# A linear-attention and expert kernel: eight input loads at the start, preparations held back behind the first block inverse, and its results sent by two queues

## The chip, the core and the metric

The kernel runs on one core of a Trainium2 chip. A core has TensorE (PE in the profile, its weight loads PEld), VectorE (DVE), ScalarE (ACT), GpSimd (POOL) and SyncE (SP), which here only issues DMAs. Each engine works through its own instructions in order; they meet through semaphores. The metric is the device time of one execution in microseconds, lower is better; several executions give a median.

## The reference

For 4 batches and 8 heads of width 40, a 40 x 40 state runs over 768 tokens; its outputs, 3072 tokens of 320 values, go into 8 experts whose weights P come from a normalised gate:

```python
for t in range(S):
    y[:, :, t] = np.einsum('bhd,bhde->bhe', rt, state)
    Sa = np.einsum('bhde,bhe->bhd', state, at)
    state_decay = state * wt[:, :, None, :] - np.einsum('bhd,bhe->bhde', Sa, bt)
    state = state_decay + np.einsum('bhd,bhe->bhde', vt, kt)
...
P = np.exp(x @ w_gate - logits.max())
for _ in range(8):
    P /= P.sum(1, keepdims=True) + 1e-09
    P /= P.sum(0, keepdims=True) + 1e-09
    P *= N / E
...
for e in range(E):
    out += P[:, e:e + 1] * (np.maximum(x @ w1[e], 0.0) @ w2[e])
```

## The kernel before

The token recurrence is done in 12 chunks of 64 tokens (`c`), for 4 batches (`b`), 8 heads as 4 pairs (`p`) with two halves (`h`). So there are 48 pieces, numbered `cb = 4c + b`. In a chunk the recurrence becomes matrix products and the inverse of a 64 x 64 unit triangular matrix for each head. Three kinds of work come of it.

*Preparation* (`prep`), one for each piece, independent of the state. It loads the packed inputs `inp` (451.5 KB), forms the running products of the decays with two scans on VectorE (`q` L124, backwards; `g` L134, forwards), stores `g` to memory as `gd`, scales keys into `kb` (L147) and `a` into `ab` (L153, L154), and forms the triangular products `ll` (L159) and the transposes `kt` (L167) on TensorE. VectorE masks a part of `ll` into `sx` (L169); ScalarE copies the rest, negated, into `lt`, which is stored to memory as `ld` (L162 or L178). From preparation 6 on, `kb` and `ab` are made by GpSimd. A set of results (`sx`, `bb`, `cc`) has 20 buffers, so that 20 preparations can be done before the recurrence has used one. Some early preparations use the memory of sets not yet needed (`IN_MAP`, `KB_SETS`, tiles called `st`) for their inputs and for `kb` and `lt`.

*Block inverse*, one for a group of two chunks (8 preparations). The triangular matrices are cut into 128 blocks of 32 x 32, one to a partition (`load_lu`, `lu`), and VectorE inverts them in place with 38 instructions, from `flip_l` (L200) over multiply and reduce pairs (`pr`, L184 to L196) to the last copy in `finish` (L369). The inverse `un` and its transpose `tn` are stored as `ud` and `nd`; `tload` brings them back by chunk as diagonal blocks `tt` (L252) and as operands `t1`, `t2` (`td`, L246, L248); `tmat` makes the off-diagonal part on TensorE (`gp` L261, `op` L266). `un`, `lu` and `tn` have one buffer each.

*Recurrence* (`recur`), five steps for each piece, with the four batches staggered: `av`, `xc`, `pu` (needs `tt` of its chunk, L308), `pm` (L310, VectorE), `c2`, `ws`, then `y`, the new state `z` and its transpose `zt`.

The events of all three are sorted by due times, and a scheduler then fixes the order on each engine; nothing is reordered at run time. The last part, the experts, has a hand-written order. Its first weights and tokens load while the recurrence ends.

The lines the change touches: the load of `inp` (L118), the buffer counts of `g1`, `q`, `kb`, `lt`, the queues of the `ld` stores, `lu` loads, `nd` stores and `tt` loads, and `do_prep`. `NSX` is 20; `N_SP = 8` says how many `ld` stores go by SP.

Of the kernel before, what the change touches and what calls it, by code (L numbers as in the profile page):

```python
# [11 lines left out]
F32 = mybir.dt.float32  # L12
# [5 lines left out]
NB, NH, S, D = 4, 8, 768, 40  # L18
C = 64
NCH = S // C  # L20
NP = 4
R2 = 104
RL = 112
# [6 lines left out]
def attention(ctx, tc, d, xd, ps, pq, pt, gs, lg):  # L30
    nc = tc.nc
    pin = ctx.enter_context(tc.tile_pool(name="a_in", bufs=1))
# [33 lines left out]
    ab_b = [pin.tile([R2, NP, 128], F32, name=f"ab{i}") for i in range(2)]  # L66
    g1_b = [pin.tile([RL, NP, 65], F32, name=f"g1{i}") for i in range(1)]
    vz_b = [const.tile([RL, NP, 104], F32, name=f"vz{i}") for i in range(5)]
# [44 lines left out]
    zp = [None] * NB  # L113

    def prep(c, b, ld):
        cb = c * NB + b
# [4 lines left out]
        a_in = inp[:, 776:1032].rearrange("r (p t) -> r p t", p=NP)  # L121
        qr = pin.tile([RL, NP, 65], F32, name="q")
        q = qr[:, ::-1]
# [3 lines left out]
        g1 = rot("g1", g1_b)  # L127
# [11 lines left out]
        if cb < NKB:  # L139
            raw = raws[KB_SETS[cb % len(KB_SETS)]]  # L140
            kb = raw[0:R2, 0:512].rearrange("r (p k t) -> r p k t", p=NP, k=2)
            lt = raw[0:64, 512:1024].rearrange("r (p k t) -> r p k t", p=NP, k=2)
        else:
            kb = pin.tile([R2, NP, 2, 64], F32, name="kb")
            lt = pin.tile([64, NP, 2, 64], F32, name="lt")
        eng = nc.vector if cb < NFAST else nc.gpsimd
# [13 lines left out]
        if cb < NKB:  # L160
            nc.scalar.activation(out=lt, in_=ll[64:128], func=AF.Copy, scale=-1.0)
            (nc.sync if cb < N_SP else nc.scalar).dma_start(out=ld[GRP[c][1], :, b], in_=lt)  # L162
            kt = pt.tile([128, NP, 2, 64], F32, name="kt", tag="pt")
        else:
            kt = pq.tile([128, NP, 2, 64], F32, name="kt", tag="pq")
# [11 lines left out]
        if cb >= NKB:  # L177
            (nc.sync if cb < N_SP else nc.scalar).dma_start(out=ld[GRP[c][1], :, b], in_=lt)  # L178
        return dict(cc=cc, g=gd, sx=sx, bb=bb)
# [53 lines left out]
    def tload(c):  # L233
        tt = rot("tt", tt_b)
        tts[c] = tt
        ld, ud, nd = invs[GRP[c][0]]
        t1, t2, lb = td_b[0][0:64], td_b[0][64:128], lg_b[0][0:64]
        cc = GRP[c][1]
        q = [slice(h * 32, h * 32 + 32) for h in range(2)]
        u = [[slice(cc * 64 + blk * 32 + h * 16, cc * 64 + blk * 32 + h * 16 + 16) for h in range(2)]  # L240
             for blk in range(2)]
        for h in range(2):
            nc.sync.dma_start(out=lb[q[h], :, q[h]],
                              in_=ld[cc, 0:32].rearrange("j b p h s -> j (b p) h s")[:, :, h, 32:64])
        for h in range(2):
            nc.sync.dma_start(out=t1[q[h]], in_=nd[u[0][h]].rearrange("g j s -> j g s"))  # L246
        for h in range(2):
            nc.sync.dma_start(out=t2[q[h]], in_=ud[u[1][h]].rearrange("g j s -> j g s"))  # L248
        for h in range(2):
            for blk in range(2):  # L250
                r = slice(h * 64 + blk * 32, h * 64 + blk * 32 + 32)
                nc.sync.dma_start(out=tt[r, :, r], in_=ud[u[blk][h]].rearrange("g j s -> j g s"))  # L252

# [107 lines left out]
    vz_cur = [rot("vz", vz_b) for _ in range(NB)]  # L361
    preps, invs, tts = {}, {}, {}

# [4 lines left out]
    def finish(s, us):  # L368
        nc.vector.tensor_copy(out=tn[us, 16:32, 0:16], in_=un[us, 0:16, 16:32].rearrange("u c j -> u j c"))  # L369
        for o in range(0, us.stop, 64):  # L370
            nc.sync.dma_start(out=invs[s][1][o:o + 64], in_=un[o:o + 64])
            nc.sync.dma_start(out=invs[s][2][o:o + 64], in_=tn[o:o + 64])

    def load_lu(s, n):
        ld = invs[s][0]
        for cc in range(n):
            for blk in range(2):
                for h in range(2):
                    u0, r0 = cc * 64 + blk * 32 + h * 16, blk * 32
                    nc.sync.dma_start(  # L380
                        out=lu[u0:u0 + 16],
                        in_=ld[cc, r0:r0 + 32].rearrange("j b p h s -> (b p) j h s")[:, :, h, r0:r0 + 32])
# [8 lines left out]
    def do_prep(s, c, b, first):  # L391
        if first:
            start_seg(s)
        preps[c, b] = prep(c, b, invs[s][0])

    for c in range(NCH):
        for b in range(NB):
            for k in range(5):
                ev.append((5 * c + k + SKEW * b, step, (c, b)))
        t = 5 * c + 2 - T_LEAD  # L400
        ev.append((t - L_LEAD, tload, (c,)))
        for half in range(2):
            ev.append((t + 2 * SKEW * half, tmat, (c, half)))
# [32 lines left out]
KB_POOL = (1,2,3,4,5,6,7)  # L436
IN_SETS = (16, 15, 14, 13)
KB_SETS = (12, 11, 10, 9)
IN_SEQ = (16,15,14,13,0,0,16,15)
IN_MAP = dict(enumerate(IN_SEQ))  # L440
N_SP = 8
NKB = 6
# [393 lines left out]
```

## Time and profile before

| what | value |
|---|---|
| median of 3 runs | 1837.33 us (1833.14 to 1839.12) |
| profiled execution, own time | 1831.31 us |
| its span | 1829.5 us |
| mean granted TensorE clock | 0.958 |
| PE busy | 1729.6 us (95%) |
| DVE busy | 1370.8 us (75%) |
| ACT, POOL busy | 855.2 us (47%), 877.5 us (48%) |
| moved by DMA | 140.47 MB |

A timeline row of the profile gives start and duration in us, engine, line, operation, output and inputs, shapes and count, and in brackets how long the engine sat idle before and what ended that. A row of grouped instructions gives the count, busy time and mean duration in ns, and the idle time before. A row of stretches gives from and to, the length, and for each engine the busy time and the number of instructions. In the page's row of slices each digit is the busy share of a fortieth of the span in tenths; for PEclk it is the clock that TensorE was granted.

### The profile page before, as it was taken

The page shows a single profiled execution, that of the slowest core. Times are in us where ns is not written, and L with a number is a line of the kernel's source. Part 1 is how long each engine was busy: PE and PEld are TensorE (multiplying, and loading weights), DVE is VectorE, ACT ScalarE, POOL GpSimd, SP SyncE. Part 2 cuts the span into 40 slices and gives each one's busy share as a digit, 9 for nine tenths or more (in the row PEclk, how much of TensorE's full clock was granted, in tenths as well). Part 3 has the DMA queues.
Part 4 walks back from the last instruction along what each step waited for, and adds up shares of the span by engine and source line. Part 5 has one row for each costly group of instructions (what it writes and reads, how often), then busy time and mean ns, then how long its engine had stood idle before and what let it go on. Part 6 is the DMA issues. An engine that isn't in the chain of part 4 may idle for free.

```text
span 1829.5 us, 31656 instructions
## 1 busy us (share of the span) xinstructions
PE 1729.6 (95%) x11843; PEld 1701.8 (93%) x11843; DVE 1370.8 (75%) x2356; ACT 855.2 (47%) x1848; POOL 877.5 (48%) x851
## 2 busy tenths in 40 slices
PE   5479999999889999999999999999999999999999
PEld 4478889889879999999999999999999999999999
DVE  7876977974798867777686878977686877767676
ACT  6347767756643533434343434345343343424342
POOL 6545655721662626547191735007182644628160
PEclk8569999989899999999999999999999999999999
DMA  7467878766620101111020112201020111102001
GB/s 193 128 150 173 191 181 178 183 139 135 176 77 20 57 20 57 38 39 57 20 75 20 57 37 61 69 1 60 16 76 20 57 38 38 57 20 75 13 26 44
DMA packets 211759, 140.47 MB, mean 77 GB/s; under 512 B 162965, under 2 KB 193813, under 8 KB 211605
## 3 DMA queue, kind: packets, MB, share of 16 engines
q1 hardware_dynamic: 207925, 132.70, 27.9%
q10 hardware_dynamic: 3680, 5.74, 1.2%
q8 instruction: 94, 1.54, 0.4%
q14 instruction: 60, 0.49, 0.1%
HBM read 110.78 MB, written 27.61 MB: 76 GB/s over the span
## 4 chain that ended last, share of the span: by engine, by line
PE 77%; DVE 6%; DMA 4%; issue 4%; POOL 2%; SPq 2%; ACT 2%; ACTq 0%; POOLq 0%; DVEq 0%
PE op L647 36%; PE p L582 33%; PE xc L297 2%; DMA inp<-in_inp_dram 1%; PE ll L159 1%; PE pu L308 1%; PE c L315 1%; PE av L289 1%; DMA xs<-xd 1%; DVE g L134 1%; POOL ab L153 1%; PE op L266 1%; DVE hl L606 1%; DVE pr L193 1%; DVE q L124 1%
## 5 line engine op out<-in xcount | busy, mean ns | idle before, releaser
L582 PE MATMUL p<-xch,wh 128*128 128x384 f32 (+1 forms) x1792 | 605.3, 339 | 9.3 <-DVE sm L600 5.6
L603 ACT ACTIVATE hh<-sm 128x384 fp32r<-128x384 f32 x512 | 269.4, 526 | 725.4 <-DVE sm L600 725.4
L647 PE MATMUL op<-wh,hh 128*128 128x320 f32 x1536 | 476.5, 311 | 1.4 <-ACT hh L603 1.3
L647 PE MATMUL op<-wl,hh 128*128 128x320 f32 x1536 | 474.3, 309 | 0.0
L647 PE MATMUL op<-wh,hl 128*128 128x320 f32 x1536 | 466.7, 309 | 0.7 <-DVE hl L606 0.7
L528 POOL TENSOR_TENSOR wl<-ws,wh 128x640 fp32r<-128x640 f32 x60 | 103.1, 1718 | 606.1 <-ACT wh L526 605.8
L606 DVE SCALAR_TENSOR_TENSOR hl<-sm,hh 128x384 fp32r<-128x384 f32 x512 | 373.0, 762 | 2.3 <-ACT hh L603 2.0
L582 PEld LDWEIGHTS p<-xch,wh 128*128 128x128 f32 (+1 forms) x1792 | 337.4, 188 | 13.1 <-DVE sm L600 6.8
L582 PE MATMUL p<-xcl,wh 128*128 128x384 f32 x896 | 302.6, 338 | 0.0
L582 PE MATMUL p<-xch,wl 128*128 128x384 f32 x896 | 301.7, 337 | 0.0
L647 PEld LDWEIGHTS op<-wh,hh 128*128 128x128 f32 x1536 | 289.9, 189 | 2.2 <-ACT hh L603 2.2
L647 PEld LDWEIGHTS op<-wl,hh 128*128 128x128 f32 x1536 | 290.7, 189 | 0.0
L647 PEld LDWEIGHTS op<-wh,hl 128*128 128x128 f32 x1536 | 286.4, 188 | 1.1 <-DVE hl L606 0.9
L600 DVE TENSOR_TENSOR sm<-p,u 128x384 f32<-128x384 f32 x384 | 234.4, 620 | 8.8
L582 PEld LDWEIGHTS p<-xcl,wh 128*128 128x128 f32 x896 | 168.8, 188 | 0.0
L582 PEld LDWEIGHTS p<-xch,wl 128*128 128x128 f32 x896 | 168.6, 188 | 0.0
L600 DVE TENSOR_TENSOR sm<-p,p 128x384 f32<-128x384 f32 x128 | 71.3, 557 | 129.0 <-PE p L582 72.4
L600 DVE TENSOR_TENSOR p<-p,p 128x384 f32<-128x384 f32 x128 | 71.1, 556 | 101.2 <-PE p L582 100.6
L600 DVE TENSOR_TENSOR u<-p,p 128x384 f32<-128x384 f32 x128 | 70.7, 553 | 58.0 <-PE p L582 56.7
L536 POOL TENSOR_TENSOR wl<-ss,wh 128x512 fp32r<-128x512 f32 x60 | 89.8, 1497 | 30.8 <-ACT wh L533 26.7
L321 POOL TENSOR_TENSOR y<-ws,gl 104x256 f32<-104x256 f32 x48 | 43.1, 897 | 121.5 <-DVE ws L317 88.7
L159 PE MATMUL ll<-ab,kb 104*128 104x128 f32 x336 | 63.0, 345 | 37.2 <-POOL kb L147 16.7
(163 smaller groups left out, 2758.0 us busy)
## 6 DMA issues: line engine op xcount, KB each, us to landing
ws<-in_wts_dram SPq DMA_DIRECT2D x60, 832.0 KB, 4.5
inp<-in_inp_dram SPq DMA_DIRECT2D x42, 451.5 KB, 4.4
gd<-g SPq DMA_DIRECT2D x48, 113.8 KB, 2.8
gl<-gd SPq DMA_DIRECT2D x48, 113.8 KB, 2.9
vz<-in_v_dram SPq DMA_DIRECT2D x48, 112.0 KB, 3.3
xd<-y SPq DMA_DIRECT2D x24, 224.0 KB, 3.5
ld<-lt ACTq DMA_DIRECT2D x40, 128.0 KB, 2.7
rb<-in_r_dram SPq DMA_DIRECT2D x96, 48.0 KB, 2.9
```

What stands on the lines that cost most here:

```text
L124: nc.vector.tensor_tensor_scan(out=qr.rearrange("r p t -> r (p t)"), data0=w65[:, 260:0:-1], data1=one65, initial=0.0, op0=ALU.mult, op1=A ...
L134: nc.vector.tensor_tensor_scan(out=ge.rearrange("r p t -> r (p t)"), data0=w65[:, 0:260], data1=g1.rearrange("r p t -> r (p t)"), initial= ...
L159: nc.tensor.matmul(ll[:, p], lhsT=kb[:, p], rhs=ab[:, p], start=True, stop=True)
L297: nc.tensor.matmul(xc[h][:, p], lhsT=pp["sx"][:, p, h], rhs=f[:, p, h], start=True, stop=True)
L321: nc.gpsimd.tensor_tensor(out=y[0:R2, :, b % 2], in0=ws[:, :, 0:64], in1=gl[0:R2, :, 0:64], op=ALU.mult)
L528: g.tensor_tensor(out=wl[:, 0:640], in0=raw[:, 256:896], in1=wh[:, 0:640], op=ALU.subtract)
L536: g.tensor_tensor(out=lv[:, 3:7], in0=so[:, :, 0], in1=hv[:, 3:7, 0], op=ALU.subtract)
L582: nc.tensor.matmul(o, lhsT=w_, rhs=x_, start=(j == 0), stop=(j == 3))
L600: eng.tensor_tensor(out=out, in0=x, in1=y, op=ALU.add)
L603: nc.scalar.activation(out=hh[:, f, h], in_=sm[f][:, h], func=AF.Relu)
L606: v.scalar_tensor_tensor(out=hl[:, f, h], in0=sm[f][:, h], scalar=0.0, in1=hh[:, f, h], op0=ALU.max, op1=ALU.subtract)
L647: nc.tensor.matmul(ops[i], lhsT=a[:, h, cs], rhs=w_[:, cw], start=(f == 0 and h == 0 and j == 0), stop=(last and h == 1 and j == 2))
```

## The change

Inputs: the first eight preparations each get a buffer of their own at the start (six in memory of sets 16, 15, 14, 13, 18, 17, two in `inp`), where six were loaded at once and the seventh and eighth waited for the first two buffers. `g1`, `q`, `kb` and `lt` have two buffers instead of one. Preparations from `N_OPEN = 10` on are issued after the last copy of the first inverse, in VectorE's order. The queue of an `ld` store is named by its group: the first group's eight go by SP, all others by ScalarE, as `N_SP = 8` had it. Of the first group's traffic, half of the `lu` loads, the `nd` stores and chunk 0's `tt` loads go by ScalarE's queue, and chunk 0 is loaded between the two halves of the results. [...]

```diff
-    g1_b = [pin.tile([RL, NP, 65], F32, name=f"g1{i}") for i in range(1)]
+    g1_b = [pin.tile([RL, NP, 65], F32, name=f"g1{i}") for i in range(2)]
...
+    def send_l(c, b, lt, ld):
+        s, cc = GRP[c]
+        (nc.scalar if s else nc.sync).dma_start(out=ld[cc, :, b], in_=lt)
...
-        qr = pin.tile([RL, NP, 65], F32, name="q")
+        qr = pin.tile([RL, NP, 65], F32, name="q", bufs=2)
...
-            kb = pin.tile([R2, NP, 2, 64], F32, name="kb")
-            lt = pin.tile([64, NP, 2, 64], F32, name="lt")
+            kb = pin.tile([R2, NP, 2, 64], F32, name="kb", bufs=2)
+            lt = pin.tile([64, NP, 2, 64], F32, name="lt", bufs=2)
...
-            (nc.sync if cb < N_SP else nc.scalar).dma_start(out=ld[GRP[c][1], :, b], in_=lt)
+            send_l(c, b, lt, ld)
...
-                nc.sync.dma_start(out=tt[r, :, r], in_=ud[u[blk][h]].rearrange("g j s -> j g s"))
+                (nc.sync if c else nc.scalar).dma_start(
+                    out=tt[r, :, r], in_=ud[u[blk][h]].rearrange("g j s -> j g s"))
...
-        nc.vector.tensor_copy(out=tn[us, 16:32, 0:16], in_=un[us, 0:16, 16:32].rearrange("u c j -> u j c"))
+        last = nc.vector.tensor_copy(out=tn[us, 16:32, 0:16], in_=un[us, 0:16, 16:32].rearrange("u c j -> u j c"))
         for o in range(0, us.stop, 64):
             nc.sync.dma_start(out=invs[s][1][o:o + 64], in_=un[o:o + 64])
-            nc.sync.dma_start(out=invs[s][2][o:o + 64], in_=tn[o:o + 64])
+            (nc.sync if s else nc.scalar).dma_start(out=invs[s][2][o:o + 64], in_=tn[o:o + 64])
+            if s == 0 and o == 0:
+                first_inv.append(last)
+                tload(0)
...
-                    nc.sync.dma_start(
+                    (nc.scalar if s == 0 and h else nc.sync).dma_start(
                         out=lu[u0:u0 + 16],
...
-        preps[c, b] = prep(c, b, invs[s][0])
+        if c * NB + b < N_OPEN:
+            preps[c, b] = prep(c, b, invs[s][0])
+        else:
+            with tc.issue_after(first_inv[0].ins):
+                preps[c, b] = prep(c, b, invs[s][0])
...
-        ev.append((t - L_LEAD, tload, (c,)))
+        if c:
+            ev.append((t - L_LEAD, tload, (c,)))
...
-IN_SETS = (16, 15, 14, 13)
+IN_SETS = (16, 15, 14, 13, 18, 17)
-IN_SEQ = (16,15,14,13,0,0,16,15)
+IN_SEQ = (16, 15, 14, 13, 18, 17, 0, 0)
-N_SP = 8
+N_OPEN = 10
...
-    nc = _bacc.Bacc("TRN2", target_bir_lowering=False, num_devices=1)
+    nc = _bacc.Bacc("TRN2", target_bir_lowering=False, num_devices=1, dynamic_dma_scratch_size=1024)
```

What the scheduler makes of it is seen on two engines. VectorE in the middle of the first inverse, before (the scans are listed as SCALAR_TENSOR_TENSOR; the line numbers after the change are 4 to 5 higher):

```order
L187 TENSOR_REDUCE un<-pr 128x4x6
L134 SCALAR_TENSOR_TENSOR g<-inp,g_205 112x260
L184 TENSOR_TENSOR pr<-un,lu 128x196
L187 TENSOR_REDUCE un<-pr 128x4x7
L169 TENSOR_TENSOR st_159<-ll,cst 64x8x64
L204 COPY tn<-un 128x4x8x8
L193 TENSOR_TENSOR pr<-un,lu 128x512
L196 TENSOR_REDUCE gt<-pr 128x64
L124 SCALAR_TENSOR_TENSOR q<-inp,cst 112x260
L193 TENSOR_TENSOR pr<-gt,tn 128x512
L128 RECIPROCAL g_205<-q 112x4
L196 TENSOR_REDUCE un<-pr 128x8x8
```

and the same stretch now:

```order
L191 TENSOR_REDUCE un<-pr 128x4x6
L188 TENSOR_TENSOR pr<-un,lu 128x196
L191 TENSOR_REDUCE un<-pr 128x4x7
L208 COPY tn<-un 128x4x8x8
L197 TENSOR_TENSOR pr<-un,lu 128x512
L200 TENSOR_REDUCE gt<-pr 128x64
L197 TENSOR_TENSOR pr<-gt,tn 128x512
L200 TENSOR_REDUCE un<-pr 128x8x8
```

The instructions of preparations have left the inverse; of all that stood there (6 `q`, 7 `g`, 7 `sx`) one `sx` remains. VectorE at the end of the first inverse, before (`st_165` is the result of preparation 16):

```order
L369 COPY tn<-un 128x16x16
L124 SCALAR_TENSOR_TENSOR q<-inp,cst 112x260
L128 RECIPROCAL g_205<-q 112x4
L134 SCALAR_TENSOR_TENSOR g<-inp,g_205 112x260
L169 TENSOR_TENSOR st_165<-ll,cst 64x8x64
L200 COPY lu<-lu 128x2x8x8
```

and now (`st_159` and `st_160` are those of preparations 10 and 11):

```order
L374 COPY tn<-un 128x16x16
L128 SCALAR_TENSOR_TENSOR q<-inp,cst 112x260 x2
L132 RECIPROCAL g_201<-q 112x4
L132 RECIPROCAL g_202<-q 112x4
L138 SCALAR_TENSOR_TENSOR g<-inp,g_201 112x260
L138 SCALAR_TENSOR_TENSOR g<-inp,g_202 112x260
L173 TENSOR_TENSOR st_159<-ll,cst 64x8x64
L128 SCALAR_TENSOR_TENSOR q<-inp,cst 112x260
L132 RECIPROCAL g_201<-q 112x4
L138 SCALAR_TENSOR_TENSOR g<-inp,g_201 112x260
L128 SCALAR_TENSOR_TENSOR q<-inp,cst 112x260
L173 TENSOR_TENSOR st_160<-ll,cst 64x8x64
```

One preparation stood between the end of the first inverse and the start of the second (L200); now ten do, 10 to 19, together with the first three `pm` of the recurrence. In the second inverse stood 5 `q`, 4 `sx` and 4 `pm`, now 9 `q`, 10 `sx` and 5 `pm`; and the third inverse, whose first copy stood three `pm` behind the second's last copy, now begins just ahead of it. SP around the last loads of the first inverse, before (`gd_568` and `gd_603` are the `g` of preparations 8 and 9; the `ld` stores shown are those of preparations 6 and 7):

```order
L178 DMA ld<-lt 64x512
L243 DMA lg<-ld 32x16x32
L138 DMA gd_568<-g 112x260
L178 DMA ld<-lt 64x512
L118 DMA inp<-in_inp_dram 112x1032
L138 DMA gd_603<-g 112x260
L380 DMA lu<-ld 16x32x32 x4
```

and now (`gd_576` and `gd_611` are those of preparations 8 and 9; the loads behind them are for 10 and 11):

```order
L117 DMA ld<-lt 64x512
L142 DMA gd_576<-g 112x260
L142 DMA gd_611<-g 112x260
L122 DMA inp<-in_inp_dram 112x1032
L117 DMA ld<-lt 64x512
L122 DMA inp<-in_inp_dram 112x1032
L388 DMA lu<-ld 16x32x32 x2
```

The store of preparation 7 has moved behind the `g` of preparation 9 and the load for preparation 10, and the last `lu` loads behind that for 11; two of the four have gone to ScalarE's queue.

More of the change, by code (lines that the diff above doesn't have):

```diff
@@ L177, in prep @@
         if cb >= NKB:
-            (nc.sync if cb < N_SP else nc.scalar).dma_start(out=ld[GRP[c][1], :, b], in_=lt)
+            send_l(c, b, lt, ld)
         return dict(cc=cc, g=gd, sx=sx, bb=bb)
@@ L361, in attention @@
     vz_cur = [rot("vz", vz_b) for _ in range(NB)]
-    preps, invs, tts = {}, {}, {}
+    preps, invs, tts, first_inv = {}, {}, {}, []
     def start_seg(s):
```

## The prediction

> **What bounds the kernel now.** I read the page's forty slices first: VectorE (DVE) is fullest and the TensorE clock lowest in the first tenth of the span, before the expert matmuls begin.
>
> ```profile
> DVE  7876977974798867777686878977686877767676
> PEclk8569999989899999999999999999999999999999
> ```
>
> Then I cut the attention stage at six rows of VectorE's timeline: start and end of the first block inverse (L200 to L369), start and end of the second, and the `pm` products that open chunk 2 and chunk 4.
>
> ```profile
> 56.32 0.27 DVE L200 COPY lu<-lu 128x128 f32<-128x128 f32 x1 [0.61 <-DMA ld<-lt]
> 97.53 0.57 DVE L369 COPY tn<-un 128x256 f32<-128x256 f32 x1
> 106.28 0.27 DVE L200 COPY lu<-lu 128x128 f32<-128x128 f32 x1 [4.23 <-DMA td<-nd]
> 148.34 0.37 DVE L369 COPY tn<-un 128x256 f32<-128x256 f32 x1
> 184.41 0.58 DVE L310 TENSOR_TENSOR pm<-pu,cst 128x416 f32<-128x416 f32 x1
> 251.89 0.56 DVE L310 TENSOR_TENSOR pm<-pu,cst 128x416 f32<-128x416 f32 x1
> ```
>
> The table of these stretches (busy time of PE, PE weight load, DVE, ACT, POOL, then granted clock, DMA share, GB/s) says which engine limits each:
>
> ```profile
> 56.30:98.10 41.80, 16.84 (x74) 14.70 (x72) 39.78 (x66) 15.75 (x40) 25.68 (x27) 0.50 0.46 125
> 98.10:106.30 8.20, 5.52 (x24) 4.90 (x24) 2.29 (x6) 3.34 (x10) 4.10 (x5) 0.50 0.84 177
> 106.30:148.70 42.40, 37.82 (x329) 35.98 (x330) 39.15 (x70) 24.43 (x61) 23.48 (x23) 0.79 0.71 148
> 148.70:184.40 35.70, 32.76 (x318) 31.24 (x317) 20.07 (x46) 24.92 (x65) 15.59 (x23) 0.97 0.77 177
> 184.40:251.90 67.50, 63.08 (x618) 60.10 (x617) 54.41 (x94) 49.92 (x126) 37.91 (x45) 0.96 0.83 188
> 251.90:420.00 168.10, 155.60 (x1442) 149.11 (x1442) 138.35 (x235) 116.32 (x295) 87.70 (x101) 0.91 0.75 166
> ```
>
> VectorE fills 95% of the first inverse and 92% of the second; from 148.7 us on TensorE is the fuller one (92%, 93%, 93%). So the first inverse is the bound where it stands, but what follows is a nearly full machine: a head start survives only as far as the work pushed behind it fits into idle time.
>
> **Step 1, until the first inverse can start** (now 56.3 us). Inputs of preparations 6 and 7 no longer wait for a buffer, and `kb`, `lt`, `q` are double. That removes two VectorE waits for `kb`, 2.02 and 1.62 us:
>
> ```profile
> 44.48 0.70 DVE L124 TENSOR_TENSOR_SCAN q<-inp,cst 112x260 f32<-112x260 f32 x1 [2.02 <-POOL kb L147]
> 48.92 0.70 DVE L124 TENSOR_TENSOR_SCAN q<-inp,cst 112x260 f32<-112x260 f32 x1 [1.62 <-POOL kb L147]
> 49.15 0.45 SPq L178 DMA_DIRECT2D ld<-lt  x1
> 51.40 1.93 SPq L380 DMA_DIRECT2D lu<-ld  x4
> ```
>
> Against it: in SP's new order the store of preparation 7 (now at 49.15) stands behind the `g` stores of 8 and 9 and the input load of 10, and the last `lu` loads behind that of 11. These wait for inputs of 8 and 9, which land 4.4 us after GpSimd has finished 6 and 7 and freed their buffers. Two of the four `lu` loads go by ScalarE's queue, half of 1.93 us. The extra `memset` of the second `g1` costs no more than the memsets in front of it, under 0.5 us. If only the gains counted the start would be 7 us earlier (49); if SP's new order eats them all, 56. I take 52, the middle: **-4**.
>
> **Step 2, the first inverse** (now 41.8 us). Its own multiply and reduce rows:
>
> ```profile
> 56.30:98.10 41.80, 24.73 (x34) 0.50 0.46 125
> ```
>
> Five transposing copies come on top, at most 0.57 each (L369), about 2.2 together, and one `sx` product (0.67) that stays between: 27.6 us. The seven preparations that shared the stretch go behind it. Bounds: 26 to 32. **-14**, so it ends at 79.6 instead of 98.1.
>
> **Step 3, from there to the second inverse** (now 8.2 us). In VectorE's new order preparations 10 to 19 all stand here, with three `pm`. One preparation, in the rows of its input tile (min/median/max ns):
>
> ```profile
> L124 DVE TENSOR_TENSOR_SCAN q<-inp,cst x42: 662/699/1187, 26.1 to 365.4; 112x260 f32<-112x260 f32 x42
> L134 DVE TENSOR_TENSOR_SCAN g<-inp,g x42: 676/698/1678, 29.3 to 369.4; 112x260 f32<-112x260 f32 x42
> L153 POOL TENSOR_TENSOR ab<-inp,g x40: 670/676/2702, 46.2 to 371.1; 40x256 f32<-40x256 f32 x40
> L154 POOL TENSOR_TENSOR ab<-inp,g x40: 673/855/2380, 47.0 to 371.8; 40x256 f32<-40x256 f32 x40
> L147 POOL TENSOR_TENSOR kb<-inp,q x40: 1171/1182/3429, 47.7 to 369.7; 104x512 f32<-104x512 f32 x40
> DMA to landing us min/median/max: 3.3/4.4/11.0
> ```
>
> There are still two `inp` buffers. A buffer goes round in 4.4 (landing) + 0.7 (`q`) + 0.7 (`g`) + 1.5 (`ab` twice) = 7.3 us, and about 8.5 with issue, reciprocal and the neighbour's 1.2 us `kb` in between. 10 and 11 are there, done 5 us after the inverse; four more pairs at 8.5 make 39; last `g` and the `lu` loads 4 more: 43 us. Lower bound, GpSimd alone: 10 x (1.18 + 0.68 + 0.86 + about 0.2) = 29. Upper bound: today's pace between 56.3 and 98.1, seven in 41.8, or 6.0 each: 60. The SP loads stand in pairs behind `g` stores, so I stay with the buffer round: **+35**. Second inverse at 122.6 instead of 106.3.
>
> Inside this step chunk 0 gets its blocks back. `nd` and the four `tt` loads go by ScalarE:
>
> ```profile
> 98.13 1.08 SPq L372 DMA_DIRECT2D nd<-tn  x2
> 105.35 2.08 SPq L252 DMA_DIRECT2D tt<-ud  x4
> 106.90 1.91 PE L261 MATMUL gp<-td,lg 64*64 64x32 f32 x16 [0.73 <-DMA td<-nd]
> 113.67 2.03 PE L308 MATMUL pu<-x,tt 128*128 128x104 f32 x8
> ```
>
> That takes 3.2 us of issue off SP, while the 16 transfer engines are at 0.84 already. But the first `pu` now stands on TensorE behind `ll` and `kt` of preparation 12, whose input is a round late, so it still comes some 16 to 19 us after the inverse, as now (15.6): it is hidden, and I cost the second queue at nothing; were that cover gone, the 3.2 us would come off step 3, and were the landings halved too, some 2 us more. [...]
>
> **Step 4, the second inverse** (now 42.4 us, 5 `q`, 4 `sx`, 4 steps inside). The new order has 9 `q`, 10 `sx` and 5 to 6 steps inside. Rows of that stretch:
>
> ```profile
> L290 DVE TENSOR_TENSOR f<-av,cst 104x512 f32<-104x512 f32 x4 | 2.7, 669 | 1.4 <-PE av L289 1.4
> L169 DVE TENSOR_TENSOR sx<-ll,cst 64x512 f32<-64x512 f32 x4 | 2.7, 667 | 0.0
> L317 DVE TENSOR_TENSOR ws<-c,c 104x416 f32<-104x416 f32 x4 | 2.3, 571 | 0.0
> L310 DVE TENSOR_TENSOR pm<-pu,cst 128x416 f32<-128x416 f32 x4 | 2.3, 563 | 0.0
> ```
>
> Added: 4 `q` and 4 `g` at 0.70, 4 reciprocals at 0.17, 6 `sx` at 0.67, one `f`, one `pm`, two `ws`: 12.7 us, about 11 after the overlap of neighbours (39.15 busy of some 44 summed). **+11**, 53 us (49 to 58).
>
> **Step 5, to chunk 2's `pm`** (now 35.7, with 15.6 us of VectorE idle). The third inverse's inputs are already there, so 23 of its rows stand here: all of its multiply and reduce rows but the twelve large ones, and a copy.
>
> ```profile
> 106.30:148.70 42.40, 24.02 (x34) 0.79 0.71 148
> L193 DVE TENSOR_TENSOR pr<-un,lu 128x1024 f32<-128x1024 f32 x3 | 3.6, 1209 | 0.0
> ```
>
> 24.0 (the second inverse's rows) - 12 x 1.2 = 9.6, the copy 0.4; 2 `q`, 4 `g`, 2 `sx` and reciprocals 6; overlapped as above 14, plus a wait that I estimate at 3 us for `un` to be stored (ending at 148.7, the store must land before the next inverse overwrites it; landings here take 3 to 4): 17 us (14 to 21). **-19**.
>
> **Step 6, to chunk 4's `pm`** (now 67.5). TensorE bounds it. Four of eight preparations are done earlier:
>
> ```profile
> 99.25 2.08 PE L159 MATMUL ll<-ab,kb 104*128 104x128 f32 x8 [4.09 <-POOL ab L154]
> 155.84 1.08 PE L159 MATMUL ll<-ab,kb 104*128 104x128 f32 x8
> 156.75 0.52 PE L167 MATMUL kt<-cst,kb 104*128 104x104 f32 x4
> ```
>
> 4 x 1.60 = 6.4 at the warm rate: **-6** (56 to 66).
>
> **Step 7, the rest.** At chunk 4 the new order has one more preparation through TensorE (1.6 us) and 12 more inverse rows plus two `q` through VectorE (about 9 us). Both engines are near full there, so between -1.6 and -9: **-5**. The experts start later or sooner by the same amount; their 1.3 ms are untouched. [...]
>
> Sum, unrounded: -4.3 - 14.2 + 34.8 + 10.6 - 18.7 - 6.4 - 5 = -3.2. Against the profiled execution's 1831.3 us that is 1828; the median before is 6 us higher, 1837.3, so **1834.0**. A difference under 0.3%, 5.5 us, can't be told from none here.
>
> **Rivals.** *The head start survives (faster).* Step 3 runs at GpSimd's pace: 33 us. For it: landings as short as 3.3 and two of every buffer; against it: SP's in-order waits. Then -13, of which the full stages keep some: 1824.
> *The held preparations are the new wait (slower).* Step 3 keeps today's 6.0 us each, 60 us, +17; chunk 2 and the third inverse follow, and later idle time gives about 5 back: 1846. It decides from 5.2 us per preparation, step 3 over 52 us. For it: today's pace, and TensorE idle and unwarmed in front of it.
> *TensorE stays cold (slower).* The granted clock is 0.50 until 106 us; 10 preparations bunched with the first steps at 2.08 instead of 1.08 for `ll` cost 1.4 us each with `kt`. Six of them on the path: +8, 1842. Against it: the clock rose to 0.79 in today's second inverse.
> *VectorE is not alone in the inverse.* `g` took up to 1678 ns against a median of 698. If GpSimd's products of preparations 8 to 10 still run beside the inverse and lengthen its rows in that way, step 2 takes its upper 32: +4, 1838, within the no-change band. [...]
>
> **Chances.** Forecast 0.40, its own range 1827 to 1841; survives 0.28; new wait 0.18; cold 0.10; not alone 0.04. Faster by over 0.3%: 0.12 of the forecast and 0.26 of the first rival, 0.38. Slower: 0.16 of the new wait, 0.05 of the cold and 0.02 of the forecast's tail, 0.23. Within: 0.39. The range reaches from the first rival's far side, 1820, to the second's, 1848, leaving 0.1 on each side.
>
> **What would show it.** L204 (L200 now) at 52; its last copy 27 us later with a single foreign row; the second inverse near 123; `pm` of chunk 2 near 193 and of chunk 4 near 253. Wrong if the ten held preparations take under 35 or over 52 us, if VectorE still idles 15 us between the second and third inverse, or if the `pu` of chunk 0 comes within 10 us of the inverse's end.

## The result, and the profile after

| what | before | after |
|---|---|---|
| median | 1836.78 us (1833.14 to 1839.12, 4 runs) | 1866.15 us (1861.72 to 1868.70, 4 runs) |
| ratio, 95% interval | | 1.0152 (1.0118 to 1.0186) |
| span of the profiled execution | 1829.5 us | 1866.8 us |
| mean granted TensorE clock | 0.958 | 0.950 |

The change makes the kernel 1.5% slower, 29 us by the medians and 37 by the two profiled executions, of which the one before lies 5 us under its median and the one after 3 us over; the forecast was 3 us faster. The slices of the page of after show the place. In the second, which holds the first inverse, GpSimd falls to 2 tenths, where it had 5 before, and the clock is at 5 as it was. In the fifth the clock is down again to 6, where it had 9:

```profile
DVE  6759758767488877686777768887676867767675
POOL 6257436551365337182553718005381835538170
PEclk9579678999979999999999999999999999999999
```

GpSimd's row before, for comparison (the other two stand in the prediction):

```profile
POOL 6545655721662626547191735007182644628160
```

The same six rows of VectorE's timeline as in the prediction (line numbers 4 to 5 higher): start and end of the first inverse, start and end of the second, the `pm` that open chunks 2 and 4.

```profile
62.06 0.27 DVE L204 COPY lu<-lu 128x128 f32<-128x128 f32 x1 [6.78 <-DMA lu<-ld]
88.50 0.37 DVE L374 COPY tn<-un 128x256 f32<-128x256 f32 x1
141.21 1.22 DVE L204 COPY lu<-lu 128x128 f32<-128x128 f32 x1 [1.25 <-DMA lu<-ld]
197.48 0.34 DVE L374 COPY tn<-un 128x256 f32<-128x256 f32 x1
221.60 0.56 DVE L315 TENSOR_TENSOR pm<-pu,cst 128x416 f32<-128x416 f32 x1
295.10 0.58 DVE L315 TENSOR_TENSOR pm<-pu,cst 128x416 f32<-128x416 f32 x1
```

The stretches between them, and the last one on to the last `pm` (busy time of PE, its weight load, DVE, ACT and POOL; then clock, DMA share, GB/s):

```profile
62.10:88.90 26.80, 0.00 (x0) 0.00 (x0) 25.66 (x41) 1.09 (x3) 0.00 (x0) 0.50 0.02 5
88.90:141.20 52.30, 40.65 (x314) 38.34 (x315) 27.26 (x45) 29.36 (x73) 31.49 (x44) 0.74 0.83 181
141.20:197.80 56.60, 42.88 (x385) 40.51 (x383) 52.32 (x94) 42.41 (x108) 37.81 (x43) 0.91 0.72 181
197.80:221.60 23.80, 17.40 (x112) 16.45 (x112) 16.04 (x36) 7.08 (x18) 9.95 (x13) 0.56 0.66 148
221.60:295.10 73.50, 68.88 (x542) 65.81 (x542) 47.64 (x86) 41.01 (x106) 25.75 (x34) 0.77 0.62 136
295.10:540.20 245.10, 226.22 (x2133) 215.99 (x2132) 169.56 (x288) 165.09 (x405) 111.95 (x130) 0.93 0.71 161
```

Read it row by row. The first inverse is as short as meant, 26.8 us, but TensorE and GpSimd do nothing at all in it (x0), and the transfer engines are 2% busy. Then VectorE, which had been the bound, is busy only 27.3 of 52.3 us, while the ten held preparations go round. The second inverse takes 56.6. Chunk 2's `pm` comes 37.2 us later than before (221.60 against 184.41), and in these two executions nothing of it comes back: the spans differ by 37.3.

The late start of the first inverse (62.06, not 56.32) has its own cause:

```profile
42.11 0.57 SPq L122 DMA_DIRECT2D inp<-in_inp_dram  x1
47.42 0.70 DVE L128 TENSOR_TENSOR_SCAN q<-inp,cst 112x260 f32<-112x260 f32 x1 [6.89 <-DMA inp<-in_inp_dram]
51.39 0.59 ACT L177 ACTIVATE lt<-ll 64x512 f32<-64x512 f32 x1 [5.68 <-DVE sx L173]
52.89 0.45 SPq L117 DMA_DIRECT2D ld<-lt  x1
```

VectorE stands 6.89 us in front of the `q` of preparation 8, whose input went out at 42.11. Behind it stands `sx` of preparation 7 (50.71), behind that ScalarE's `lt` of 7, and behind that, at 52.89, the last store that the inverse needs. That store goes out 3.7 us later than before (49.15); the other 2.0 us of the late start lie behind it, where it takes 4.1 us to land and the last `lu` loads 4.2 to 4.4.

### The profile page after: what moved, and what is told of

Same layout as the page of the kernel before. It is cut to its first block, busy times and chain, and to the rows that moved or that the text cites. A ratio compares the mean times of both kernels' runs of the same rounds, so it can differ in the third digit from the quotient of the medians.

```text
span 1866.8 us, 31645 instructions
## 1 busy us (share of the span) xinstructions
PE 1739.9 (93%) x11843; PEld 1712.9 (92%) x11843; DVE 1366.1 (73%) x2357; ACT 855.6 (46%) x1848; POOL 865.9 (46%) x851
## 4 chain that ended last, share of the span: by engine, by line
PE 73%; DVE 3%; DMA 1%; issue 1%; POOL 0%; SPq 0%; ACT 0%; DVEq 0%; ACTq 0%; POOLq 0%
PE op L660 35%; PE p L595 33%; PE xc L302 1%; PE pu L313 1%; PE c L320 1%; PE av L294 1%; DVE hl L619 1%; PE op L271 0%; DVE sm L613 0%; DMA ws<-in_wts_dram 0%; PE zt L340 0%; PE gp L266 0%; PE lp L350 0%; DMA inp<-in_inp_dram 0%; DVE u L613 0%
## 5 line engine op out<-in xcount | busy, mean ns | idle before, releaser
L163 PE MATMUL ll<-ab,kb 104*128 104x128 f32 x336 | 59.6, 329 | 66.2 <-POOL ab L158 55.5
L163 PEld LDWEIGHTS ll<-ab,kb 104*128 104x128 f32 x336 | 51.4, 232 | 70.0 <-POOL ab L158 57.2
```

The lines of the kernel that those rows point to most:

```text
L163: nc.tensor.matmul(ll[:, p], lhsT=kb[:, p], rhs=ab[:, p], start=True, stop=True)
```

## The experiments

All times are medians, the ratios against the kernel before, run beside each. The columns: start of the first inverse, first `pm` of chunk 2, and from chunk 4's first `pm` to the last (length and granted clock), all from the one profiled execution of each, so that some us of a stretch can be that execution's own. Each kernel also has its own order from the scheduler; where two kernels differ by a few us, that order can be the reason as well as the edit's own subject, and no run separates the two.

| kernel | median us | ratio (95%) | inverse 1 | chunk 2 | chunk 4 to last |
|---|---|---|---|---|---|
| before | 1836.8 | | 56.3 | 184.4 | 248.8 at 0.91 |
| after | 1866.2 | 1.0152 (1.0118 to 1.0186) | 62.1 | 221.6 | 245.2 at 0.93 |
| hold_alone | 1844.9 | 1.0048 (1.0024 to 1.0073) | 56.1 | 209.9 | 239.7 at 0.92 |
| no_hold | 1842.7 | 1.0033 (1.0016 to 1.0050) | 59.5 | 196.1 | 251.8 at 0.91 |
| hold_from_16 | 1845.3 | 1.0051 (1.0031 to 1.0071) | 59.2 | 192.2 | 252.5 at 0.91 |
| hold_from_8 | 1865.0 | 1.0161 (1.0136 to 1.0186) | 51.8 | 222.9 | 242.9 at 0.93 |
| one_queue | 1874.9 | 1.0190 (1.0155 to 1.0225) | 61.9 | 227.3 | 248.3 at 0.91 |
| hold_8_behind_flip | 1876.1 | 1.0202 (1.0170 to 1.0233) | 53.5 | 225.2 | 257.7 at 0.87 |
| start_first_no_hold | 1854.0 | 1.0086 (1.0053 to 1.0118) | 51.8 | 195.3 | 256.3 at 0.86 |
| fill_idle | 1863.0 | 1.0128 (1.0101 to 1.0155) | 60.8 | 222.5 | 243.2 at 0.92 |
| queue_alone | 1839.6 | 1.0012 (0.9993 to 1.0031) | 56.7 | 183.4 | 256.4 at 0.88 |
| eight_loads_alone | 1852.9 | 1.0090 (1.0071 to 1.0109) | 58.4 | 192.8 | 249.5 at 0.92 |
| single_buffers | 1843.0 | 1.0030 (1.0011 to 1.0049) | 59.1 | 211.9 | 237.2 at 0.93 |
| three_inputs | 1865.9 | 1.0170 (1.0148 to 1.0193) | 59.6 | 218.0 | 263.0 at 0.85 |
| qg_double | 1867.8 | 1.0152 (1.0112 to 1.0191) | 60.6 | 219.4 | 260.2 at 0.87 |
| kb_lt_double | 1852.0 | 1.0071 (1.0043 to 1.0099) | 56.0 | 214.9 | 241.1 at 0.94 |
| no_hold_single | 1851.9 | 1.0076 (1.0050 to 1.0101) | 57.7 | 190.4 | 256.7 at 0.90 |
| hold_and_queue | 1849.9 | 1.0072 (1.0049 to 1.0095) | 56.3 | 207.6 | 241.6 at 0.92 |
| fill_longer | 1872.1 | 1.0172 (1.0136 to 1.0207) | 61.7 | 221.9 | 254.0 at 0.90 |
| hold_from_13 | 1844.1 | 1.0031 (1.0012 to 1.0051) | 57.3 | 195.5 | 248.1 at 0.89 |

**Which half of the change costs.** *no_hold*, the change with nothing held:

```diff
-N_OPEN = 10
+N_OPEN = 48
```

> The whole change but the hold (N_OPEN = 48: no preparation waits for the first inverse). Theory A, the ten held preparations that run at 5.2 us each between the inverses are the cause: without them the time goes back to 1830 to 1843, the first inverse is long again (about 40 us, preparations inside) and the second begins within 10 us of its end. Theory B, the new start (eight loads at once, pairs of q and g in front of the first inverse) is the cause, since the first inverse begins at 62.1 where it began at 56.3: the time stays at 1855 or more. Theory C, the second queue and chunk 0 first: stays at 1855 or more too. Both A and B expect the first inverse to begin at 60 to 63.

*hold_alone*, the kernel before with only the hold:

```diff
-        preps[c, b] = prep(c, b, invs[s][0])
+        if c * NB + b < N_OPEN:
+            preps[c, b] = prep(c, b, invs[s][0])
+        else:
+            with tc.issue_after(first_inv[0].ins):
+                preps[c, b] = prep(c, b, invs[s][0])
```

> The kernel before with the hold alone (preparations 10 on behind the first inverse's last copy); inputs, buffers and queues as before. Theory A: the first inverse begins near 56, lasts 27, the second begins 45 to 55 us behind its end, and the time is 1855 to 1870. Theories B and C: within 5 us of the time before, 1832 to 1842.

Neither theory holds alone. Without the hold 1842.7, the hold alone 1844.9: 6 and 8 us, where both together make 29. The rows say where they add and where they don't. Timeline of hold_alone:

```profile
82.51 0.37 DVE L369 COPY tn<-un 128x256 f32<-128x256 f32 x1
133.39 0.27 DVE L200 COPY lu<-lu 128x128 f32<-128x128 f32 x1 [3.13 <-DMA lu<-ld]
209.91 0.58 DVE L310 TENSOR_TENSOR pm<-pu,cst 128x416 f32<-128x416 f32 x1
```

and of no_hold:

```profile
196.05 0.56 DVE L315 TENSOR_TENSOR pm<-pu,cst 128x416 f32<-128x416 f32 x1
```

Theory A's forecast for no_hold came true (1830 to 1843); for hold_alone the time lies between the forecasts. Up to chunk 2's `pm` the two add up in these executions: 25.5 us from the hold (209.91 - 184.41), 11.6 from the rest, 37.2 together in after. With the old buffers and inputs the hold's ten preparations also take 50.5 us (82.9 to 133.4), nearly as long as in after. What differs is behind: the kernel with the hold alone wins 8 us back in the rest of the recurrence (308.3 us from chunk 2's `pm` to the last, before 316.3), after loses 2 more (318.7).

*hold_from_16* and *hold_from_8*, other limits of the hold in the change:

```diff
-N_OPEN = 10
+N_OPEN = 16   # hold_from_8: 8
```

> The change with the hold from preparation 16 on (N_OPEN = 16), so that the second inverse's own eight preparations stand beside the first inverse and the second begins right behind it in VectorE's order. Theory A in the form that the ten preparations bunch between the two inverses: most of the loss goes, 1830 to 1845. Theory A in the form that any idling of TensorE and GpSimd during the first inverse costs: 1845 to 1860. Theories B and C: 1855 or more.

> The change with the hold from preparation 8 on (N_OPEN = 8): twelve preparations held, and nothing of 8 and 9 in front of the first inverse. Theory A: two more held at 5.2 us, less some 5 us from an earlier first inverse (its last stores no longer stand behind q and g of 8 and 9): 1866 to 1876, the first inverse at 52 to 57. Theory B: the start is mended, and the time falls by what the inverse begins earlier, to 1856 to 1862.

From 16 on the second group stands beside the first inverse again, chunk 2 comes at 192.2, and the time is that of no hold, at the edge of what the bunching form of theory A forecast (1830 to 1845): the bunching between the inverses is what the hold costs. From 8 on the first inverse begins at 51.75, as theory B wanted, and yet the time is that of the change, 1865.0: the two more preparations take the 10 us back before the second inverse (145.8). It lies between the forecasts of A (1866 to 1876) and B (1856 to 1862).

**Whether the late start is what costs.** *hold_8_behind_flip* and *start_first_no_hold*:

```diff
+        fl = nc.vector.tensor_copy(out=lh[:, :, 8:16, 0:8], ...)   # in flip_l
+        if not first_flip:
+            first_flip.append(fl)
...
+        if c * NB + b < 8:
+            preps[c, b] = prep(c, b, invs[s][0])
+        elif c * NB + b < N_OPEN:      # 10; start_first_no_hold: 48
+            with tc.issue_after(first_flip[0].ins):
+                preps[c, b] = prep(c, b, invs[s][0])
...
```

> The change, but preparations 8 and 9 are issued behind the first copy of the first inverse (they stand inside it), 10 on behind its end as in the change. Theory D, a late start costs its full length once the held preparations stand behind it (start 6 us late here, and only there): the first inverse begins at 51 to 53, as with the hold from 8, ends at 80 to 84, the second begins near 132 instead of 141, and the time is 1852 to 1860. Rival, the loss sits in the ten preparations and in what follows whatever the start: 1863 or more.

> The change's loads, buffers and queues without the hold; preparations 8 on are only kept behind the first copy of the first inverse. Theory D: the early start (51 to 53, before 56) is kept through a first inverse of 42 to 46 with preparations inside, the second begins at 97 to 101 (before 106), and of the 5 us some survive: 1830 to 1838. Rival, any early crowding of VectorE is paid back later, as without the hold: 1840 to 1846.

Theory D falls. The first inverse begins at 53.5 and 51.8, 9 and 10 us earlier than in after, and the times are 1876.1 and 1854.0. With the hold the second inverse still begins at 138.9; without it the first lasts to 104 and the second begins only at 120.7. An earlier first inverse is worth nothing here: in VectorE's order the second inverse stands behind the rows of its own eight preparations. Without the hold the time is over both forecasts (1840 to 1846 was the higher); why stays open.

**The second queue.** *one_queue* is the change on SP alone, *queue_alone* the kernel before with the second queue and chunk 0 first:

```diff
-                (nc.sync if c else nc.scalar).dma_start(          # tt; nd and lu alike
+                nc.sync.dma_start(
```

> The change with its second queue undone: nd stores, lu loads and chunk 0's tt loads go by SP again, chunk 0 still first. Theory A (hold and late start together) has no part in the queue: within 6 us of the change, 1860 to 1872, the first pu of chunk 0 no more than 4 us later. Theory C (the second queue disturbs ScalarE's work): 1850 or less.

> The kernel before with the second queue and chunk 0 first alone: no hold, inputs and buffers as before. In the change the second queue was worth some 9 us (without it 1874.9). If that is issue time saved on SP it counts here too: 1828 to 1834, the second inverse begins 3 to 5 us behind the end of the first sooner than before's 8.2. Rival, it counts only behind the hold, where SP is crowded: 1834 to 1842, no difference.

Alone it changes nothing that can be measured (1.0012, 0.9993 to 1.0031). In the change it looks worth 9 us, but the intervals overlap (1.0155 to 1.0225 against 1.0118 to 1.0186). With 1874.9 one_queue lies 3 us over its forecast; in neither place does the second queue show a cost, so it is no cause of the loss.

**Loads and buffers.** *eight_loads_alone*, the kernel before with the new input memory (`IN_SETS` and `IN_SEQ` of the change); *single_buffers*, the change without its second buffers:

```diff
-IN_SEQ = (16,15,14,13,0,0,16,15)
+IN_SEQ = (16, 15, 14, 13, 18, 17, 0, 0)     # eight_loads_alone
...
-        qr = pin.tile([RL, NP, 65], F32, name="q", bufs=2)
+        qr = pin.tile([RL, NP, 65], F32, name="q")    # single_buffers; g1, kb, lt alike
```

> The kernel before with the eight early loads alone (sets 18 and 17 lend memory); single buffers of q, g, kb and lt, one queue, no hold. Theory F, the pairs that double buffers make in VectorE's order (q q g g) are what costs in the new start, and the loads by themselves help: the first inverse begins at 52 to 55 (before 56.3), 1830 to 1836. Rival G, the loads themselves cost (the first inputs arrive later behind two more): 1840 or more.

> The change with single buffers of q, g, kb and lt again; eight loads, hold and second queue stay. Theory F: the first inverse begins before 58 instead of 62, the held stretch loses its pairs, and the time comes down to that of the hold alone, 1842 to 1852. Rival G: 1860 or more.

*single_buffers* is the run that splits the loss. Eight loads, the hold and the second queue with single buffers take 1843.0; the second buffers add 23 us, over three quarters of the loss. Its time is theory F's, though the first inverse begins at 59.1 and not before 58. The loads by themselves cost 16 us, as rival G had it and clear of noise: 1852.9 (1.0071 to 1.0109). Chunk 2 comes 8 us later there, and the stretch to chunk 4 takes 77.8 us at a clock of 0.80, before 67.5 at 0.96. Behind the hold this cost is not seen (see hold_and_queue below). So the change's loss is not laid to the loads; alone they are a loss of their own, and its cause stays open.

Which buffers: *qg_double* doubles `q` and `g1` alone, *kb_lt_double* `kb` and `lt`, and *no_hold_single* has no hold and no double buffers:

```diff
+        qr = pin.tile([RL, NP, 65], F32, name="q", bufs=2)     # qg_double, with two g1
+            kb = pin.tile([R2, NP, 2, 64], F32, name="kb", bufs=2)   # kb_lt_double, with lt
```

> The change with kb and lt single again, q and g double. If the pairs q q g g on VectorE, which put the last stores of the first group behind inputs 8 and 9, are what costs: the first inverse begins at 60 to 62 and the time stays at 1858 to 1868. If kb and lt do it, through the two more preparations ahead of chunk 2's first pu on TensorE (here only one more, 28, where single buffers have 27 and the change 29): 1842 to 1850.

> The change with q and g single again, kb and lt double; 29 preparations stand ahead of chunk 2's first pu as in the change, and VectorE's pairs are gone. If kb and lt do it: the second inverse lasts 55 us or more, TensorE's clock is low between the first pm of chunk 2 and that of chunk 4, 1856 to 1868. If the pairs do it: 1842 to 1850.

> The change without the hold and with single buffers: eight loads, second queue, chunk 0 first. If double buffers cost only behind the hold: within 6 us of the change without the hold, 1837 to 1849. If single buffers are better everywhere: 1830 to 1836, and this is the best of all.

`q` and `g1` bring the whole loss back, 1867.8; `kb` and `lt` give 1852.0, an interval (1.0043 to 1.0099) that touches that of single buffers (1.0011 to 1.0049): their part isn't settled. Without the hold the sign turns: all four single 1851.9, over both forecasts, and all four double 1842.7 (the intervals meet at 1.0050). So with the hold two buffers for `q` and `g1` lose; without it, two buffers for all four gain. Which of the four gain there was not tried.

Where the 25 us of qg_double go is seen in two stretches, from chunk 2's first `pm` to chunk 4's and from there to the last. single_buffers:

```profile
211.90:278.30 66.40, 59.86 (x590) 57.06 (x589) 48.00 (x87) 46.60 (x117) 26.05 (x38) 0.95 0.72 159
278.30:515.60 237.30, 222.14 (x2115) 213.29 (x2115) 172.91 (x291) 164.61 (x404) 112.56 (x130) 0.93 0.73 168
```

qg_double:

```profile
219.40:281.00 61.60, 57.92 (x575) 54.91 (x575) 44.41 (x82) 41.40 (x105) 25.87 (x34) 0.99 0.69 151
281.00:541.20 260.20, 242.75 (x2141) 231.63 (x2139) 175.01 (x299) 167.97 (x413) 111.93 (x133) 0.87 0.69 157
```

7.5 us are lost before chunk 2, 4.8 won up to chunk 4, 22.9 lost behind it. There both do nearly the same matrix products (2115 and 2141 records, of which some can be missing), TensorE is 93 to 94% busy in both, and the longer one has the lower clock: length times clock is 237.3 x 0.93 = 221 and 260.2 x 0.87 = 226. In after, against single_buffers, it is 9.7 before chunk 2, 7.1 up to chunk 4 (542 products in 73.5 us at 0.77, 590 in 66.4 at 0.95) and 7.9 behind. Over all 20 kernels the last column of the table has this form: 2113 to 2143 products, length times clock 220 to 231, lengths from 237 to 263.

**The pace of the held preparations.** *three_inputs*:

```diff
-... pin.tile([RL, 1032], F32, name="inp", bufs=2)
+... pin.tile([RL, 1032], F32, name="inp", bufs=3)
```

> The change with three input buffers instead of two. Theory H, the round of the two input buffers sets the pace of the held preparations (5.2 us each): the stretch from the end of the first inverse to the second's start falls from 52.3 to 40 to 46, the time to 1854 to 1862. Rival, SP's in-order issue (loads behind the g stores) and GpSimd set it: 50 to 54, 1863 to 1870.

From 85.9 to 134.1, 48.2 us instead of 52.3, between the two forecasts, and the time, 1865.9, is the rival's: the buffer round is a part, not the bound. In after, VectorE's largest waits in that stretch are five for inputs, and SP has seven for `g` (sum, times, longest):

```profile
DVE q L128 <- DMA inp<-in_inp_dram: 17.9, 5, 5.3
```

```profile
SPq L142 <- DVE g L138: 17.6, 7, 4.2
```

The loads stand on SP behind `gd` stores that wait for `g`; VectorE stands before the next `q`, waiting for such a load. With three buffers the transfer share is 0.95 there (0.83 in after), and whether the transfers are the next bound no run shows. The 4 us don't last: the stretch from chunk 4 on is the longest of all these kernels.

```profile
277.80:540.80 263.00, 244.67 (x2141) 233.63 (x2141) 170.82 (x286) 164.52 (x406) 112.83 (x128) 0.85 0.66 147
```

**Hold without the rest.** *hold_and_queue* (the kernel before, hold and second queue) and *hold_from_13* (the kernel before, `N_OPEN = 13`), whose edits stand above:

> The kernel before with the hold, the second queue and chunk 0 first; six early loads and single buffers as before. If the eight loads have no part behind the hold: that of the change with single buffers, 1840 to 1847. If they cost, as alone (16 us): 1830 to 1837. If they help: 1848 or more.

> The kernel before with a milder hold: preparations 13 on behind the first inverse (10 to 12 stand inside it again, seven bunch behind it), all else as before. The hold from 10 cost 25 us until chunk 2's first pm and got 8 to 10 of it back in the recurrence. If both shrink with the number held: 10 to 12 us later at chunk 2's pm, 5 back, 1838 to 1845. If the gain in the recurrence comes whole and the cost shrinks: 1828 to 1835, better than before.

Both are slower than before (1849.9, 1844.1). The eight loads are no harm behind the hold: single_buffers has them and takes 1843.0, less than hold_and_queue without them, with intervals that meet at 1.0049. A milder hold costs 11 us at chunk 2 and wins nothing later. No version beat the kernel before.

**Clock, cause or company.** *fill_idle* gives TensorE something to do in its idle 9.9 us before preparation 27's `ll`, *fill_longer* fills them whole:

```diff
+        if cb == FILL_AT:                                  # 27
+            dm = pq.tile([128, 512], F32, name="dm", tag="pq")
+            for _ in range(N_FILL):                        # 7; fill_longer: 13
+                nc.tensor.matmul(dm, lhsT=ident, rhs=cst[:, 0:512], start=True, stop=True)
```

> The change with seven matrix products that nobody reads (128x128 by 512 columns, about 1.3 us each at full clock, worked out from pu's 1.1 us for four of 104 columns) in TensorE's idle 9.9 us between 191.6 and 201.4, in front of preparation 27's ll. Theory E, the granted clock of 0.50 behind that idle time costs part of what follows: the clock stays near 1.00 from 201 to 220, chunk 2's first pm comes 3 to 6 us earlier than 221.6, and the time falls by 3 to 10 us, to 1856 to 1863. Rival, the waits for td and tt loads set that stretch whatever the clock: within 2 us, 1864 to 1868.

> The change with thirteen unread products of 512 columns in front of preparation 27's ll instead of the seven of the first fill, whose rows gave 0.90 us each at full clock: 11.7 us, from 192.8 to some 204.5, so that no idle time is left before the ll at 202.9. If the clock is a cause: it stays at 1.00 from 193 to 218, TensorE does the ten groups there in 1.0 instead of 2.0 us each, chunk 2's first pm comes at 214 to 219 instead of 221.6, and the time falls to 1852 to 1862. If it is only company (the loads of td and tt, and VectorE behind them, set the pace): pm at 221 to 224, 1862 to 1869.

Theory E missed in both: chunk 2's `pm` came no earlier, at 222.5 and 221.9. Fill_idle's 1863.0 is at the very edge of E's range, fill_longer's 1872.1 over both ranges, and neither time differs from the change's beyond the intervals. Filled in fill_longer, the clock stayed at 0.99 to 1.00 from 194.2 to 209.5, but `gp` still waited for `td` until 207.8 and the clock fell to 0.50 anyway. The last wait in front of `pm` is not TensorE's at all: VectorE stands 4.68 us before a `q`, until 216.46, for an input; `pu` is done at 217.7, and `pm` follows in VectorE's order at 221.85. That stretch is set by the loads. So the longer stages go with a lower clock, but that the clock is their cause isn't shown; the gaps behind which it fell may be.

## Why the prediction was wrong, by its own steps

| step | forecast | measured | missed by |
|---|---|---|---|
| 1, to the first inverse | -4.3 | +5.7 | 10.0 |
| 2, first inverse | -14.2 | -15.0 | -0.8 |
| 3, to the second inverse | +34.8 | +44.1 | 9.3 |
| 4, second inverse | +10.6 | +14.2 | 3.6 |
| 5, to chunk 2's `pm` | -18.7 | -11.9 | 6.8 |
| 6, to chunk 4's `pm` | -6.4 | +6.0 | 12.4 |
| 7, the rest | -5 | -5.9 | -0.9 |
| sum | -3.2 | +37.2 | 40.4 |

The measured column is the difference of the two profiled executions, so that up to 8 of the 37 us can be theirs alone. Steps 1, 3, 5 and 6 failed, step 6 by the most; step 4 was sized too low.

*Step 1* failed in its mechanism. It saw the store of preparation 7 behind SP's new loads and took the middle of its two ends; it missed that on VectorE `sx` of 7 stands behind `q` and `g` of 8 and 9, so that the new inputs' landing comes into the chain. With nothing of 8 and 9 in front the start was at 51.8 (hold_from_8): the 52 was right for another order. Its early end, 7 us, is also more than the gains it prices, 3.6 us of waits and 1.0 of issue, and its late end, 56, was no bound.

*Step 2* was right to a microsecond, and it was the wrong thing to win. The stretch had been full of other work (PE 16.8, POOL 25.7 us); what it saved came back in step 3, in hold_alone too (an inverse of 26.8 us, then 50.5).

*Step 3* had the mechanism right and the size wrong: 52.3 us, 5.2 each, exactly where the second rival was said to decide. The forecast rested on the round of two buffers, at 8.5 us a pair, and left SP's waits for `g` (17.6 us above) out of it; three_inputs shows that this is a part of it only, and hold_alone, with other buffers, has 50.5. The truth lay midway between the pace built from parts (4.3) and that measured in the old stretch (6.0).

*Step 4* counted the rows nearly right and sized them too low. VectorE's busy time in the second inverse grew by 13.2 us (39.15 to 52.32), where 10.6 was forecast: `q` and `g` took 837 and 792 ns, where 700 was counted, and the third inverse's first copies (1.0 us) stand inside too.

```profile
L128 DVE TENSOR_TENSOR_SCAN q<-inp,cst 112x260 f32<-112x260 f32 x9 | 7.5, 837 | 4.0 <-DMA inp<-in_inp_dram 3.9
L138 DVE TENSOR_TENSOR_SCAN g<-inp,g 112x260 f32<-112x260 f32 x7 | 5.5, 792 | 0.0
```

The rest of the miss, 1.0 us, is idle time (3.2 us before, 4.3 after). The wait for inputs grew, from the first of these lines to the second; before, 1.4 us for `av` came on top.

```profile
DVE q L124 <- DMA inp<-in_inp_dram: 1.4, 1, 1.4
DVE q L128 <- DMA inp<-in_inp_dram: 3.9, 5, 1.2
```

*Step 5* left out a wait. Its 14 us of VectorE's rows were 16.0, and the 3 us for `un` to be stored were 2.7, but VectorE's idle time was 7.8 us in all: it also stood 1.2 us for an `ll` and 3.2 us for an input. That input, not `pu`, is what chunk 2's `pm` came behind. `pu` was done at 216.3; `pm` stands behind this `q` and the rows that follow it, and began at 221.60.

```profile
214.28 2.01 PE L313 MATMUL pu<-x,tt 128*128 128x104 f32 x8
215.36 0.70 DVE L128 TENSOR_TENSOR_SCAN q<-inp,cst 112x260 f32<-112x260 f32 x1 [3.24 <-DMA inp<-in_inp_dram]
```

*Step 6* missed by the most: it took the rate of its rows at 155.84 and 156.75 (1.60 us for `ll` and `kt`), from a stretch with a clock of 0.97. The clock was 0.77 here, and 542 products kept TensorE busy for 68.9 us, where 618 took 63.1 before. Where the clock stayed at 0.97 to 0.99, the stretch took what the step forecast, 61: 59.7 us in three_inputs and 61.6 in qg_double. "TensorE stays cold" stood among the rivals with 0.10, but it was looked for only up to the second inverse. It came behind it.

*Step 7* was right in sum, though the trade inside it (inverse rows against one preparation) wasn't tested.

Of the rivals, the new wait and the cold TensorE came together; the prediction priced each alone, at +17 and +8, as if they excluded each other. And the second buffers were counted as a gain of two `kb` waits in step 1. That they would be three quarters of the loss was in no rival. That they cost by way of the order which they let the scheduler choose, `q q g g`, is argued and not shown: no run has two buffers with the order of one. Why the clock late in the recurrence is lower with two `q` (0.87 in qg_double, 0.93 in single_buffers) stays open. That GpSimd's products lengthen VectorE's rows, as the last rival had it, is not shown: beside the first inverse of after GpSimd had none (x0).

The second queue was costed at nothing; alone, that is what it measured (1.0012). No run here separates saved issue time from no effect. Nor does a run show what `dynamic_dma_scratch_size=1024` does: no kernel has it alone.

## What to carry to other kernels

Before clearing work out of an engine's critical stretch, ask who needs the cleared work next: here the second inverse needed it, and 15 us won in the inverse came back as 44 behind it, since work that had stood side by side now stood one after the other. When edits come in a bundle, run them in parts and combinations: parts that cost 6 and 8 us cost 29 together, and second buffers that gain in one order lose in another. Price the work of a nearly full TensorE with the granted clock of its own stretch: here 542 products took 68.9 us at 0.77, where 618 had taken 63.1 at 0.96.

## What the runs showed of the hardware

In these traces the clock fell behind gaps of 1.2 to 1.4 us, and stayed down for up to 16 us of work. Rows of after, from 221 us:

```profile
221.00:222.00 1.00, 0.00 (x0) 0.00 (x0) 1.00 (x3) 0.90 (x2) 0.93 (x2) 0.99 0.00 0
222.00:225.00 3.00, 2.78 (x16) 2.73 (x17) 2.93 (x5) 2.65 (x8) 2.62 (x3) 0.50 0.68 173
225.00:230.00 5.00, 4.49 (x46) 4.14 (x45) 4.44 (x7) 0.87 (x3) 0.19 (x1) 0.96 0.89 188
230.00:233.00 3.00, 1.80 (x14) 1.66 (x15) 3.00 (x6) 0.57 (x2) 2.55 (x3) 0.87 0.66 130
233.00:249.00 16.00, 16.00 (x85) 15.06 (x84) 10.56 (x15) 9.71 (x25) 4.81 (x6) 0.50 0.44 96
```

At 222 it fell behind 1.4 us without products, and at 232 with 1.2 us of idle time in the three from 230 on. It was back after 3 us the first time, and only after 16 us the next, with TensorE shown busy for 16.00 of them. In fill_longer it stood at 1.00 through 11.4 us of unbroken products and at 0.99 in the next 3.9, which hold 1.4 us of idle time; then it was at 0.50 for ten:

```profile
194.20:205.60 11.40, 11.40 (x28) 5.18 (x29) 7.72 (x18) 2.77 (x7) 6.88 (x8) 1.00 0.79 209
205.60:209.50 3.90, 2.49 (x28) 2.06 (x27) 3.66 (x10) 0.55 (x2) 0.00 (x0) 0.99 0.79 125
209.50:219.50 10.00, 9.78 (x56) 9.72 (x57) 5.25 (x11) 3.52 (x9) 2.00 (x2) 0.50 0.66 145
```

The length of the gap alone doesn't decide in these rows. In fill_idle the clock held at 1.00 through 3.8 us without a product, and fell only 1 us into the work that followed:

```profile
199.10:202.90 3.80, 0.00 (x0) 0.00 (x0) 2.29 (x5) 0.42 (x2) 3.68 (x5) 1.00 0.93 216
202.90:204.00 1.10, 1.10 (x10) 1.10 (x11) 0.16 (x1) 0.75 (x2) 1.00 (x2) 0.99 1.02 202
204.00:212.00 8.00, 5.94 (x39) 5.27 (x38) 6.61 (x18) 3.79 (x10) 0.36 (x1) 0.50 0.85 157
```

Cut into rows of half a microsecond, after shows the clock from 217 to 255 us at 0.50 or 1.00 in 71 of 76, and each of the other five stands beside a change. No one length of gap or of work goes with all of them: the falls came behind 1.2 to 1.4 us of idle time and, in fill_idle, 1.1 us into the work behind 3.8; the returns came after 3, 10 and 16 us. Of the 85 products in those 16 us 22 are small (`lp` has 8 columns, `gp` 32), the others have 104 or 128; why the clock stayed at 0.50 through them is open.

The clock also goes with the time where no instruction differs: over 91 executions of the kernel before, 1831.7 to 1849.7 us, the mean clock runs from 0.960 to 0.943, 9.6 us for each 0.01 (correlation -0.74). Which of the two moves the other is not shown by that.
